# Last thirds of q and k in fewer transfers, and one closing barrier, in a cross-covariance attention kernel

## The chip, the cores and the metric

The kernel runs on one core of a Trainium2 chip. The metric is the time of one execution on the device in microseconds (us). The core has a matrix engine (PE, with its weight loads shown as PEld), a vector engine (DVE), an engine for activations and copies (ACT), GpSimd (POOL) and SyncE (SP). Sixteen DMA engines move data between the device's memory (DRAM) and the on-chip buffers. Each compute engine runs its own list of instructions in order, and engines wait for each other, and for transfers, through semaphores.

## The reference

The inputs q, k and v have shape (4, 6400, 256): four batches of 6400 rows (tokens) and 256 channels. First comes an attention over channels:

```python
qn = q / (np.linalg.norm(q, axis=1, keepdims=True) + 1e-06)
kn = k / (np.linalg.norm(k, axis=1, keepdims=True) + 1e-06)
s = kn.transpose(0, 2, 1) @ qn / tau          # 256 x 256 for each batch
s = s - s.max(-1, keepdims=True)
a = np.exp(s)
a /= a.sum(-1, keepdims=True) + 1e-09
x = v @ a                                      # 6400 x 256 for each batch
```

Then a mixture of eight experts of rank 16 is added. `w_gate` is (256, 8), `A` is (8, 256, 16), `B` is (8, 16, 256), and every row of x uses its two best experts:

```python
logits = x @ w_gate
topk = np.argpartition(-logits, K, axis=1)[:, :K]     # K = 2
w = softmax of the two chosen logits
out = x + sum over the two experts of w * ((x @ A[e]) @ B[e])
```

The 256 x 256 matrix of a batch needs all 6400 rows of q and k of that batch, so no row of the output can be computed before all of q and k of its batch has been read.

## The kernel before

**Tiles.** The 6400 rows of a batch lie on 128 partitions as 50 columns, each a row of 256 channels on every partition. A batch's q and k come in three thirds of 17, 17 and 16 columns (`QK`), its v in five pieces of 10 columns (`V`). POOL issues the loads of q, k and v, which cast from f32 to bf16 on the way, by one line, L562. The first four columns of q and k of batch 0 are an exception: SP and ACT load them as f32 (L558) and ACT casts them (L758). Of some thirds, `PARTS` cuts the transfer further:

```python
QK = ((0, 17), (17, 17), (34, 16))
PARTS = {(0, 0): ((0, 2), (2, 15)), (0, 2): ((34, 8), (42, 5), (47, 3)), (3, 2): ((34, 8), (42, 5),
        (47, 3))}
```

So the last third (columns 34 to 49) of q and of k comes in transfers of 8, 5 and 3 columns in batches 0 and 3, and in one transfer of 16 columns in batches 1 and 2.

**Stages of a batch.** For each column PE adds k'q to two accumulators (step G, L577). The squared norms of q and k come either from PE too (k'k at L581, q'q at L586) or, for the groups of columns listed in `OFF`, from ACT and DVE: ACT squares the group (L599), DVE adds it to a running sum (L605), halves that sum at the end (L611, L614), and PE sums it over the partitions (L620). After the last column ACT copies the accumulators (L635), DVE takes the diagonals (L647), computes reciprocal square roots (L661 to L677), PE spreads the scale of q (L689), ACT does the exponentials (L699), PE transposes (L713) and multiplies with the gate's and the experts' weights (L726, L729), and DVE scales the result (L741, L747). From there on the pieces of v can be turned into output: PE transposes a piece (T, L772), computes logits and expert inputs (L796, L810, L863), DVE and ACT compute the gate (L829 to L852, L874), PE transposes the gated values (L886), and the output is the sum of two products (Y, L899 and L904), which ACT or DVE copies to the tile y (L753, L755). SP stores it (L912). T and the loads of v need nothing of the attention; the other steps on v do.

**What sets the order.** A planner (`Plan.run`) plays the whole program once with assumed durations when the kernel is built, and the instructions are written in the order in which it started the steps. Each engine takes, of its ready steps, the one with the lowest rank; the steps from the last column of q and k to the scaled weights have ranks near -100 and go first. Loads go in the fixed order of `WORDS`, in which `q12` is third 2 of q and k of batch 1, and `v12` piece 2 of v of batch 1. A load starts when its buffer is free; there are six buffers for thirds of q or k and three for pieces of v. At most eight loads are outstanding: they take eight semaphores in turn, and a load waits until the load eight places before it has landed. Where the planner finds PE idle for long it puts warm-up products in (L761), which nothing reads. SP's stores of the earlier batches are held back by tiny transfers (L629) that wait until certain loads have landed (`HOLD`).

**The end.** When the kernel's function is done, the compiler's framework appends a closing block. SP waits there for all semaphores of transfers and engines. Then all engines meet in a barrier: the others raise a gather semaphore, POOL waits for all four, and raises a release semaphore that the others wait for. POOL then drains, clears the range of semaphores that the program used, and all engines meet in a second barrier of the same kind. `nc.at_finalize` lets a kernel edit the finished list of instructions, and the function `first_ahead` uses it for the first two loads.

Of the kernel before, what the change touches and what calls it, by code (L numbers as in the profile page):

```python
# [230 lines left out]
def make_plan(B, order, ahead):  # L231
# [6 lines left out]
    for kind, b, i in order:  # L238
        if kind == "v":
            p.add(("load", "v", b, i, V[i][0] * PC, V[i][1] * PC), {}, (), 0, take=(("v", (b, i)),),  # L240
                  size=LOAD * V[i][1] * PC + 0.062)
            continue
        for c, n in PARTS.get((b, i), QK[i:i + 1]):
            for h in "qk":
                p.add(("load", h, b, i, c, n), {}, (), 0, take=(("qk", (h, b, i)),), size=LOAD * n + 0.062)

    for h in "qk":
        p.add(("cast", h), {"ACT": 0.6}, [("load", h, 0, 0) + PARTS[0, 0][0]], 0)
    p.loads[2].size += 0.5
    for b in range(B):  # L250

        for i, (c0, n) in enumerate(QK):
            for c in range(c0, c0 + n):
                deps = [k for k in p.steps if k[0] == "load" and k[2:4] == (b, i) and k[1] != "v"
                        and k[4] <= c < k[4] + k[5]]
                if (b, c) < (0, PARTS[0, 0][0][1]):
                    deps = [("cast", k[1]) for k in deps]
# [32 lines left out]
        if b == 0:  # L290
            p.add(("wts",), {"DVE": 1.8}, [("load", "k", 0, len(QK) - 1) + PARTS[0, len(QK) - 1][1]], -200)

# [101 lines left out]
def make_order(words):  # L394

    order = [("qk", 0, i) for i in range(len(QK))]
    for w in words.split():
# [12 lines left out]
        (1, 1): ('k', 3, 2), (1, 2): ('k', 3, 2), (1, 3): ('k', 3, 2), (1, 4): ('k', 3, 2),  # L410
        (2, 0): ('k', 3, 1), (2, 1): ('k', 3, 2), (2, 4): ('k', 3, 1)}

PARTS = {(0, 0): ((0, 2), (2, 15)), (0, 2): ((34, 8), (42, 5), (47, 3)), (3, 2): ((34, 8), (42, 5),
        (47, 3))}
FINE = 2
FIRST = 4
OFF = {(0, 0, 'k'), (0, 0, 'q'), (0, 1, 'q'), (0, 2, 'k'), (0, 2, 'q'), (0, 4, 'q'), (0, 5, 'q'),
# [10 lines left out]
def first_ahead(nc, names):  # L428


    def move(nc):
        main, body = nc.main_func.blocks[:2]
        first = [i for i in body.instructions if i.name in names]
        assert len(first) == len(names), (names, len(first))
        rest = [i for i in body.instructions if i.name not in names]
        at = next(n for n, i in enumerate(main.instructions) if type(i).__name__ == "InstMemset")
        main.instructions = main.instructions[:at] + first + main.instructions[at:]
        body.instructions = rest
    nc.at_finalize(move)


@with_exitstack
def kernel(
# [11 lines left out]
    nc = tc.nc  # L455
# [42 lines left out]
    def make_consts():  # L498
        ident = const.tile([P, P], BF16, name="ident")
        make_identity(nc, ident)  # L500
        W["ident"] = ident
        W["ident32"] = const.tile([P, P], FP32, name="ident32")
        nc.vector.tensor_copy(W["ident32"], ident)
        ones = const.tile([P, P], FP32, name="ones")
        nc.vector.memset(ones, 1.0)
        W["ones"] = ones
        neg = const.tile([P, 1], FP32, name="neg_inv_tau")
        nc.vector.memset(neg, -inv_tau)
        W["neg"] = neg
        W["zeros"] = const.tile([P, 256], BF16, name="zeros")  # L510
        nc.vector.memset(W["zeros"], 0.0)
        nc.scalar.activation(scrap[:, 0:1], neg[0:1, :], ACT.Exp)
# [413 lines left out]
    for s in steps:  # L926
        do[s.key[0]](s, *s.key[1:])
        if s.key[0] == "load":
# [3 lines left out]
            if n_load == 4:  # L932
                make_consts()
    first_ahead(nc, {i.ins.name for i in early})


# [33 lines left out]
```

## Time and profile before

| what | value |
|---|---|
| time, median of 4 runs | 254.81 us (254.69 to 254.83) |
| time of the profiled execution | 254.82 us |
| its span, first to last instruction | 253.0 us |
| PE busy, share of the span | 217.5 us, 86% |
| DVE busy | 193.1 us, 76% |
| ACT busy | 150.6 us, 60% |
| loads of q and k, 1088 KB each | 14 issues by POOL, 23.4 us (q) and 28.1 us (k) from issue to landing |
| loads of 320 KB (5 columns) | 4 issues, 21.6 us (q) and 24.4 us (k) |
| loads of 192 KB (3 columns) | 4 issues, 22.9 us (q) and 21.6 us (k) |
| one DMA issue on POOL | 0.53 us |

The span is what the instructions of the program cover; the execution's time is longer by the work around it. The times from issue to landing include the time that a transfer waits behind others in the queue. Sizes of loads are given as they are read (f32); a page's GB/s and MB for a queue count what is written (bf16 for the casting loads). A slice of the page is a fortieth of the span, 6.3 us.

### The profile page before, as it was taken

The page shows a single profiled execution, that of the slowest core. Times are in us where ns is not written, and L with a number is a line of the kernel's source. Part 1 is how long each engine was busy: PE and PEld are TensorE (multiplying, and loading weights), DVE is VectorE, ACT ScalarE, POOL GpSimd, SP SyncE. Part 2 cuts the span into 40 slices and gives each one's busy share as a digit, 9 for nine tenths or more (in the row PEclk, how much of TensorE's full clock was granted, in tenths as well). Part 3 has the DMA queues.
Part 4 walks back from the last instruction along what each step waited for, and adds up shares of the span by engine and source line. Part 5 has one row for each costly group of instructions (what it writes and reads, how often), then busy time and mean ns, then how long its engine had stood idle before and what let it go on. Part 6 is the DMA issues. An engine that isn't in the chain of part 4 may idle for free.

```text
span 253.0 us, 5843 instructions
## 1 busy us (share of the span) xinstructions
PE 217.5 (86%) x2343; PEld 192.6 (76%) x2343; DVE 193.1 (76%) x527; ACT 150.6 (60%) x270; POOL 30.2 (12%) x58
## 2 busy tenths in 40 slices
PE   0273993899999998899999999989999869999980
PEld 0162882588989996699889998779999759999970
DVE  0055589879899978898989995689888878988920
ACT  5354436546766645877667548443776746647680
POOL 7001220040020002000030100510000210000000
PEclk9999799799999999999999999999999999999998
DMA  8999999999999999999999999999999999999995
GB/s 247 213 217 211 211 222 209 216 221 212 219 211 211 320 294 294 257 212 223 208 217 221 215 215 219 210 210 353 279 286 313 335 317 315 322 419 427 422 408 217
DMA packets 11819, 66.70 MB, mean 264 GB/s; under 512 B 1424, under 2 KB 2320, under 8 KB 7184
## 3 DMA queue, kind: packets, MB, share of 16 engines
q0 software_dynamic: 7488, 38.80, 74.6%
q1 hardware_dynamic: 3968, 26.87, 26.1%
q10 hardware_dynamic: 336, 0.66, 0.8%
q8 instruction: 18, 0.29, 0.4%
q14 instruction: 9, 0.07, 0.1%
HBM read 78.91 MB, written 26.21 MB: 415 GB/s over the span
## 4 chain that ended last, share of the span: by engine, by line
DMA 46%; PE 45%; DVE 3%; POOL 2%; issue 1%; ACT 0%; POOLq 0%
DMA qk<-in_k_dram 21%; DMA v<-in_v_dram 20%; PE Y_ps L899 12%; PE acc L577 6%; PE T_ps L772 6%; PE Y_ps L904 6%; DMA qk<-in_q_dram 4%; PE gzT_ps L886 4%; PE ZL_ps L796 3%; PE acc L586 2%; PE acc L581 2%; PE Z_ps L863 2%; POOL qk L562 1%; PE log_ps L810 1%; DVE a_bf L747 1%
## 5 line engine op out<-in xcount | busy, mean ns | idle before, releaser
L577 PE MATMUL acc<-qk 128*128 128x256 bf16 x400 | 71.4, 286 | 18.4 <-DMA qk<-in_k_dram 11.4
L605 DVE TENSOR_TENSOR ssq<-ssq,sq 128x1280 f32<-128x1280 f32 (+1 forms) x27 | 43.4, 1607 | 22.6 <-ACT sq L599 20.6
L899 PE MATMUL Y_ps<-a_bf,vT 128*128 128x256 bf16 x400 | 60.0, 273 | 0.0
L753 ACT COPY y<-Y_ps 128x512 f32<-128x512 f32 x79 | 46.0, 587 | 18.6 <-PE Y_ps L904 15.8
L599 ACT ACTIVATE sq<-qk 128x1280 f32<-128x1280 bf16 (+1 forms) x27 | 36.9, 1367 | 26.4 <-DVE ssq L605 19.7
L577 PEld LDWEIGHTS <-qk 128*128 128x128 bf16 x400 | 34.9, 103 | 22.9 <-DMA qk<-in_k_dram 13.6
L899 PEld LDWEIGHTS <-vT 128*128 128x128 bf16 x400 | 38.9, 98 | 3.9
L904 PE MATMUL Y_ps<-ball,gzT 128*128 128x256 bf16 x200 | 38.2, 273 | 0.3 <-DVE gzT L755 0.3
L581 PE MATMUL acc<-qk 128*128 128x128 bf16 x242 | 34.8, 226 | 0.0
L772 PE MATMUL T_ps<-ident,v 128*128 128x128 f32 x200 | 27.1, 276 | 1.6 <-DVE gatemask L839 0.9
L562 POOL DMA_DIRECT2D v<-in_v_dram x20 | 12.2, 612 | 128.8 <-PE T_ps L772 81.8
L581 PEld LDWEIGHTS <-qk 128*128 128x128 bf16 x242 | 24.5, 101 | 3.7
L753 ACT COPY vT<-T_ps 128x512 f32<-128x512 f32 (+1 forms) x44 | 21.7, 516 | 9.2 <-PE T_ps L772 8.8
L874 DVE TENSOR_TENSOR gz<-zl,gateg 128x256 bf16<-128x256 f32 x70 | 26.0, 446 | 0.3
L772 PEld LDWEIGHTS T_ps<-ident,v 128*128 128x128 f32 x200 | 22.3, 143 | 3.1 <-DMA v<-in_v_dram 1.1
L586 PE MATMUL acc<-qk 128*128 128x128 bf16 x168 | 23.6, 223 | 0.0
L904 PEld LDWEIGHTS <-gzT 128*128 128x128 bf16 x200 | 19.4, 98 | 3.0 <-DVE gzT L755 0.6
L796 PE MATMUL ZL_ps<-waA_sb,vT 128*128 128x136 bf16 x280 | 19.6, 222 | 1.3 <-DVE waA_sb L741 0.9
L886 PE MATMUL gzT_ps<-ident,gz 128*128 128x128 f32 x100 | 20.4, 278 | 0.0
L796 PEld LDWEIGHTS <-vT 128*128 128x128 bf16 x280 | 17.8, 98 | 2.1 <-issue 1.7
L755 DVE COPY gzT<-gzT_ps 128x256 f32<-128x256 f32 (+1 forms) x39 | 14.9, 390 | 4.5 <-PE gzT_ps L886 4.0
L599 ACT ACTIVATE ssq<-qk 128x1536 f32<-128x1536 bf16 x8 | 11.9, 1484 | 8.1 <-DMA qk<-in_q_dram 3.9
(80 smaller groups left out, 269.8 us busy)
## 6 DMA issues: line engine op xcount, KB each, us to landing
out_dram<-y SPq DMA_DIRECT2D x18, 1280.0 KB, 17.9
v<-in_v_dram POOLq DMA_DIRECT2D x20, 640.0 KB, 20.5
qk<-in_q_dram POOLq DMA_DIRECT2D x7, 1088.0 KB, 23.4
qk<-in_k_dram POOLq DMA_DIRECT2D x7, 1088.0 KB, 28.1
qk<-in_q_dram POOLq DMA_DIRECT2D x2, 1024.0 KB, 18.2
qk<-in_k_dram POOLq DMA_DIRECT2D x2, 1024.0 KB, 22.7
out_dram<-y SPq DMA_DIRECT2D x4, 512.0 KB, 6.2
qk<-in_q_dram POOLq DMA_DIRECT2D x2, 512.0 KB, 16.9
```

The source lines that it names most:

```text
L577: nc.tensor.matmul(acc[ic][:, 0:256], kt[:, j, ic::CC], qt[:, j, :], start=c == 0, stop=False, skip_group_check=True)
L581: nc.tensor.matmul(acc[ic][:, 256:384], kt[:, j, ic::CC], kt[:, j, ic::CC], start=False, stop=False, skip_group_check=True)
L586: nc.tensor.matmul(acc[ic][:, 384:512], qt[:, j, ic * P:(ic + 1) * P], qt[:, j, ic * P:(ic + 1) * P], start=False, stop=c == NC - 1, skip_ ...
L599: nc.scalar.activation(out[:, 0:n, :], t[:, j:j + n, :], ACT.Square)
L605: nc.vector.tensor_tensor(out=t, in0=t, in1=held["sq", (w, b, g), ""][:, 0:n, :], op=OP.add)
L753: nc.scalar.copy(out, in_)
L772: nc.tensor.matmul(ps[:, j, :], vt[:, c + j, :].bitcast(FP32), W["ident32"], is_transpose=True, start=(j == 0), stop=(j == n - 1))
L796: nc.tensor.matmul(ps[:, j, :], vT_of(b, i, c + j)[:, :, ic], st[b]["waA"][:, ic, :], start=(j == 0 and ic == 0), stop=(j == n - 1 and ic ...
L874: nc.vector.tensor_tensor(out=pairs[:, h].rearrange("p c (e r) -> p c e r", e=E), in0=z[:, 2 * h:2 * h + 2, :].rearrange("p c (e r) -> p c ...
L886: nc.tensor.matmul(ps[:, j, :], pairs[:, j * P:(j + 1) * P], W["ident32"], is_transpose=True, start=(j == 0), stop=(j == n // 2 - 1))
L899: nc.tensor.matmul(ps[:, j, :], vT_of(b, i, c + j)[:, :, ic], st[b]["a"][:, ic, :], start=(j == 0 and ic == 0), stop=False, skip_group_che ...
L904: nc.tensor.matmul(ps[:, j, :], pair[:, :, j], W["B"], start=False, stop=(j == 1), skip_group_check=True)
```

## The change

Two edits. First, `PARTS`: the last thirds of q and k in batches 0 and 3 come in two transfers of 8 columns each, in place of 8, 5 and 3. Second, a new function `one_end_barrier` edits the closing block: it removes POOL's release of the first barrier, all of the second barrier of the other engines, and POOL's gather wait of the second, so that POOL gathers, drains, clears the semaphores, drains and then releases the others once.

```diff
-PARTS = {(0, 0): ((0, 2), (2, 15)), (0, 2): ((34, 8), (42, 5), (47, 3)), (3, 2): ((34, 8), (42, 5),
-        (47, 3))}
+PARTS = {(0, 0): ((0, 2), (2, 15)), (0, 2): ((34, 8), (42, 8)), (3, 2): ((34, 8), (42, 8))}
...
+def one_end_barrier(nc):
+
+
+    def trim(nc):
+        end = nc.main_func.blocks[-1]
+        ins = list(end.instructions)
+        pool = [n for n, i in enumerate(ins) if i.engine == mybir.EngineType.Pool]
+        clear = next(n for n in pool if type(ins[n]).__name__ == "InstISA")
+        before = [n for n in pool if n < clear and type(ins[n]).__name__ == "InstEventSemaphore"]
+        after = [n for n in range(clear + 1, len(ins))]
+        release = [n for n in after if n in pool and type(ins[n]).__name__ == "InstEventSemaphore"]
+        assert len(before) == 2 and len(release) == 2 and len(after) == 11, (before, release, after)
+        drop = {before[-1]} | {n for n in after if n != release[-1] and n != release[0] - 1}
+        end.instructions = [i for n, i in enumerate(ins) if n not in drop]
+    nc.at_finalize(trim)
...
             if n_load == 4:
                 make_consts()
     first_ahead(nc, {i.ins.name for i in early})
+    one_end_barrier(nc)
```

The planner reads `PARTS`, so the order of the program changes too. In the built program POOL has four loads fewer, PE 14 warm-up products more (2337 products in place of 2323), and from the end of batch 0's columns on the lists of PE, DVE and ACT differ in most places. At the end of batch 0, ACT now copies the first accumulator before its last square rather than after it, DVE takes the diagonals before the two reductions rather than between them, and PE adds 12 columns of batch 1 rather than 5 before it spreads the scale of q. On SP the first store goes ahead of the first holding transfer, and the third holding transfer goes ahead by one store.

## The prediction

> **What bounds the kernel now.** I read first the page's second and third parts (the span in 40 slices, and the DMA queues).
>
> ```profile
> span 253.0 us, 5843 instructions
> ...
> DMA  8999999999999999999999999999999999999995
> GB/s 247 213 217 211 211 222 209 216 221 212 219 211 211 320 294 294 257 212 223 208 217 221 215 215 219 210 210 353 279 286 313 335 317 315 322 419 427 422 408 217
> ...
> q0 software_dynamic: 7488, 38.80, 74.6%
> q1 hardware_dynamic: 3968, 26.87, 26.1%
> ...
> HBM read 78.91 MB, written 26.21 MB: 415 GB/s over the span
> ```
>
> The DMA row is full in every slice but the first and the last. The casting loads (q0) and the stores (q1) together hold 74.6 + 26.1 = 100.7% of the sixteen engines' span. The drop from 420 to 210 GB/s is no idling: a casting load reads four bytes for each two that it writes, and only the written ones are counted. So no wait elsewhere sets the end unless it leaves the DMA queue empty.
>
> Second, the busy time by stage, for who sets the last microseconds.
>
> ```profile
> core 0: us, PE busy (x) PEld busy (x) DVE busy (x) ACT busy (x) POOL busy (x), PEclk, DMA share, GB/s
> ...
> 24.00:36.00 12.00, 11.46 (x118) 10.36 (x119) 7.43 (x13) 5.51 (x4) 3.36 (x6) 0.86 1.09 214
> 36.00:60.00 24.00, 18.82 (x193) 14.98 (x191) 20.62 (x59) 13.33 (x22) 3.47 (x5) 0.93 1.04 215
> 224.00:246.00 22.00, 21.73 (x237) 19.66 (x235) 16.54 (x56) 15.91 (x33) 0.00 (x0) 1.00 1.00 419
> 246.00:248.00 2.00, 0.00 (x0) 0.00 (x0) 0.00 (x0) 0.35 (x1) 0.00 (x0) 1.00 1.02 409
> 248.00:250.00 2.00, 0.00 (x0) 0.00 (x0) 0.00 (x0) 0.00 (x0) 0.00 (x0) 1.00 0.77 311
> 250.00:252.00 2.00, 0.00 (x0) 0.00 (x0) 0.00 (x0) 0.00 (x0) 0.00 (x0) 0.64 0.28 112
> ```
>
> PE works to the last product (it ends at 245.74), the last store is issued at 246.38, and then the DMA engines run down unevenly: all busy to 248, 0.77 of them to 250, 0.28 to 252. In the trace's landing records the sixteen completions of that last store come in from 248.87 to 252.14. The quickest engines thus had nothing queued before it; the slowest was still 252.14 - 248.87 = 3.27 us behind, with DMA work alone. So the slowest engine's queue sets the end, and PE has about 3.3 us in hand.
>
> Third, the closing rows and the waits of POOL, which issues all loads but the first two.
>
> ```profile
> L965 POOLq EVENT_SEMAPHORE  x4: 17/17/17, 252.3 to 252.9; - x4
> L965 POOLq DRAIN  x3: 40/93/19034, 207.0 to 252.8; - x3
> ...
> POOL v L562 <- PE T_ps L772: 81.8, 10, 20.6
> POOL qk L562 <- ACT ssq L599: 16.6, 1, 16.6
> ```
>
> POOL waits long for buffers, but with transfers queued behind it: at 158.17, after its 16.6 us for ACT, a k transfer of 1088 KB was still due to land at 166.81; the shortest cover I found is at 198.83, where the transfer before landed at 205.26, 6.4 us later.
>
> **The change, part by part.** The sum is made against the profiled execution: 254.82 us, span 253.04, so 1.78 around it; the median of the runs is 254.81, the same.
>
> *Closing barrier.* Starts from the trace, POOL's sequencer: gather wait 252.314, release 252.392, drain 252.473, range clear 252.595, drain 252.768, second gather wait 252.853, release 252.931; the other engines take the release from 252.973 and the span ends at 253.036. The edit takes two links out of this chain: the first release (252.392 to 252.473, 0.08) and the second gather wait (252.853 to 252.931, 0.08). Nothing runs beside them. The other engines' second drains were over by 252.61, ahead of POOL: nothing. Sum: -0.16 us. Bounds 0 (should the last drain wait longer) and -0.24 (a third such link).
>
> *Four transfers fewer.* 5 + 3 columns in two transfers become 8 in one, for q and k, in batches 0 and 3. The bytes stay. Removed are 4 x 128 = 512 packets, 512/16 = 32 per engine. In the trace's packet records a packet of 2560 written bytes takes 211 ns, one of 1536 takes 135, one of 4096 on the same queue 324: 211 + 135 - 324 = 22 ns, times 32 = 0.70 us. That is the upper bound, because packets overlap: the window of 24 to 36, where the small ones run, shows a DMA share of 1.09. The landings give the net price. Back to back, 10 columns (v, 640 KB) come 3.04 us apart, and 17 columns (1088 KB) 5.18: (5.18 - 3.04)/7 = 0.306 a column, leaving 3.04 - 3.06 = nothing per transfer. Batch 0's two small pieces of q and of k, 16 columns in four transfers, took 5.01 us (first completions, from 28.54 of the transfer before to 33.55 of the last); 16 x 0.306 = 4.90. Four transfers cost 0.11 there, and two fewer save about half, 0.06; I allow 0.07 for each batch. Sum: -0.14, bounds 0 and -0.70. I take the landings over the packet times, since they are what a waiting engine sees.
>
> The Trainium skill, "DMA: Bandwidth & Descriptors", section "Anatomy of one DMA", gives each GpSimd-issued transfer a fixed 2.0 us besides its bytes; charged in full for four transfers it would be an estimate of 8 us and a time near 246.7. The spacing above shows no such charge while the queue is full, so the measurement decides and the rule counts only for a lone transfer.
>
> *POOL's issues.* Four DMA issues of 0.53 us fall away, and two waits: before, the fifth transfer of q in batch 0 (issued 10.51) and of k (14.46) waited for a free semaphore of eight; now eight transfers are issued at once. Later loads wait for an earlier neighbour by two. But the next q load at 20.48 waits for its buffer (PE), unchanged, and the queue is full until 35. Worth nothing, hidden by 14 us of queued transfers.
>
> *Later data.* Columns 42 to 46 of k now arrive with 47 to 49, near 34.9 instead of 33.16. PE then has 8 columns of 0.33 us (the 28.85 to 32.5 rows) ahead of it: 34.9 + 2.7 + 0.3 for the start = 37.9, against 37.3 now. In the changed program ACT's copy of the accumulator stands ahead of the last square, so that square moves from 37.58 to about 38.4. On DVE the diagonal sums (0.84) and the two reductions (1.84 each) follow in another order; the row scales, ready at 47.3 now, come near 48.3: +1.0 us for batch 0's softmax. Its cover: at 50.44, when the next v load is issued, transfers are queued until 64.90. In batch 3, column 42 starts near 181 and the last column ends at 192.9, while all of q and k has landed at 183.40: PE's order decides there, not the landing. Nothing on the path, as long as PE ends before 245.74 + 3.27 = 249.0.
>
> *New order.* The planner moves most instructions of PE, DVE and ACT after batch 0, and puts in 14 more warm-up products. Six of them take 1.46 us at 40.01 (0.22 from start to start): 14 x 0.22 = 3.1 if they stand before waiting work, nothing if PE is idle there; most stand in the wait for batch 0's sums (PE busy 18.82 of 24.00 in 36 to 60). I take 0 to 1 us on PE, inside the 3.3.
>
> Total: 254.82 - 0.16 - 0.14 = 254.52, so **254.5**; its own range 253.96 (both full) to 254.66 (barrier alone).
>
> **Rivals.**
>
> *The packets pay in full.* For it: 32 packets less on every engine, and the slowest engine sets the end. Against it: the share over 1, which says that a packet's fixed part runs under its neighbour. 254.82 - 0.16 - 0.70 = 253.96.
>
> *PE becomes the bound at the end.* The mechanism: a PE that starts batch 0's output later stays late, because it is full afterwards (21.73 of 22.00 in the stage above), and the last store is issued after the slowest engine would have run dry. It decides from a PE end of 249.0. Its price: 1.0 for the chain, 3.1 for the warm-up products if they all stand before work, makes 4.1, or 0.8 past the cover; if the five later columns also cost batch 3 their 5 x 0.44 = 2.2 (the spacing of full columns at 172.33 to 174.55), 3.0. Less the barrier: 255.5 to 257.7, of which I take 255.5. For it: the changed order of everything. Against it: PE sits idle for 2.2 us in 200 to 210, which can take up lateness.
>
> *Nothing happens.* The queue's gain is lost in the uneven run-down of the engines and the last drain takes the barrier's: 254.8. For it: a single 16 KB instruction fetch takes 0.9 us of one engine, as much as the whole gain.
>
> **How the numbers follow.** This kernel's measurement can tell about 0.2% (0.51 us) from no change: faster is below 254.30, slower above 255.32. My forecast has 0.38, packets in full 0.33, PE bound 0.22, nothing 0.07. The forecast and nothing lie within 0.2% but for 0.02 at the fast edge: faster 0.35, same 0.43, slower 0.22. The range starts below the full packets by the run-down's play of 0.25 and ends at the PE rival's near price: 253.7 to 255.6.
>
> **What would show it.** Barrier right: one release in the closing rows, and 0.73 us in place of 0.89 from the last landing to the end of the span. Packets: four fewer landings, and the last q and k of batch 0 landing 0.05 to 0.35 us sooner than 35.01. Cover right: the DMA share at 0.99 or more up to 246, and PE's end below 249.0. Wrong: a stage with a DMA share under 0.97 before 246, a last completion that comes in with the first (PE bound), or a batch 0 chain late by more than 3 us.

## The result and the profile after

| | before | after |
|---|---|---|
| time, median | 254.78 us (61 runs, 254.60 to 254.93) | 254.39 us (41 runs, 254.21 to 254.65) |
| span of the profiled execution | 253.04 us | 252.56 us |
| last landing | 252.14 | 251.83 |
| end of PE's last product | 245.7 | 246.3 |

The ratio is 0.9985, with a 95% interval from 0.9981 to 0.9990: 0.39 us less, between 0.26 and 0.48. Forecast were 254.5, 0.30 us less than before, and a range from 253.7 to 255.6. The spans, landings and ends of PE in the table are those of one profiled execution of each kernel.

The page of the kernel after, its DMA rows:

```profile
span 252.6 us, 5852 instructions
...
DMA  8999999999999999999999999999999999999996
GB/s 253 210 218 209 215 224 209 212 224 214 214 213 213 319 292 290 263 213 221 210 215 217 218 219 215 211 212 318 312 253 342 332 332 316 347 385 428 406 408 242
DMA packets 11244, 66.70 MB, mean 264 GB/s; under 512 B 1361, under 2 KB 1745, under 8 KB 6609
...
q0 software_dynamic: 6912, 38.80, 74.4%
```

The same bytes move in 7488 - 6912 = 576 packets fewer: the 512 that carry data and 64 completions. The queue's own time falls from 74.6% of 253.04 to 74.4% of 252.56 us. The DMA row is as full as before.

The closing rows of the kernel after (instructions of one line: engine, count, shortest, middle and longest time in nanoseconds, first and last start; the lines of this kernel are numbered 16 or 17 higher than those of the kernel before):

```profile
L982 POOLq DRAIN  x3: 40/102/13032, 213.2 to 252.4; - x3
L982 SPq DRAIN  x2: 7/7/7, 251.9 to 252.0; - x2
L982 POOLq EVENT_SEMAPHORE  x2: 17/17/17, 252.0 to 252.5; - x2
```

POOL has two semaphore instructions there in place of four. From the last landing to the end of the span it is 252.56 - 251.83 = 0.74 us, where it was 0.89.

The stage from 238 to 240 of the kernel before, and the last stages of the kernel after (busy us of each engine, clock, DMA share, GB/s):

```profile
238.00:240.00 2.00, 2.00 (x21) 1.72 (x19) 1.99 (x7) 0.82 (x3) 0.00 (x0) 1.00 1.02 424
```

```profile
238.00:240.00 2.00, 2.00 (x27) 1.87 (x25) 2.00 (x7) 0.96 (x2) 0.00 (x0) 1.00 0.87 363
...
246.00:248.00 2.00, 0.32 (x3) 0.04 (x1) 0.00 (x0) 0.87 (x2) 0.00 (x0) 1.00 1.03 407
248.00:250.00 2.00, 0.00 (x0) 0.00 (x0) 0.00 (x0) 0.00 (x0) 0.00 (x0) 1.00 0.83 334
250.00:252.00 2.00, 0.00 (x0) 0.00 (x0) 0.00 (x0) 0.00 (x0) 0.00 (x0) 0.56 0.20 78
```

PE ends 0.6 us later than before, and at 238 to 240 the DMA engines were not all busy (0.87, where it was 1.02). Yet the last landing is 0.31 us earlier. The sixteen completions of the last store come in from 249.48 to 251.83, 2.35 us apart where it was 3.27. The first of them comes 2.5 us after the store is issued in both kernels (246.38 to 248.87, 246.97 to 249.48), so the narrower distance follows PE's later end; the slowest engine did not lose by it.

### The profile page after: what moved, and what is told of

It reads as the page before. It is cut to its first block, busy times and chain, and to the rows that moved or that the text cites. A ratio compares the mean times of both kernels' runs of the same rounds, so it can differ in the third digit from the quotient of the medians.

```text
span 252.6 us, 5852 instructions
## 1 busy us (share of the span) xinstructions
PE 221.1 (88%) x2357; PEld 195.2 (77%) x2357; DVE 192.8 (76%) x528; ACT 151.2 (60%) x269; POOL 27.1 (11%) x54
## 3 DMA queue, kind: packets, MB, share of 16 engines
q0 software_dynamic: 6912, 38.80, 74.4%
## 4 chain that ended last, share of the span: by engine, by line
PE 76%; DVE 9%; DMA 8%; ACT 2%; issue 2%; POOL 1%; DVEq 0%; POOLq 0%
PE Y_ps L915 17%; PE acc L593 16%; PE Y_ps L920 8%; DMA qk<-in_k_dram 8%; PE T_ps L788 7%; PE ZL_ps L812 6%; PE gzT_ps L902 5%; PE acc L597 5%; PE acc L602 4%; PE warm_ps L777 2%; PE n2p_ps L636 2%; DVE a_bf L763 2%; PE Z_ps L879 1%; PE log_ps L826 1%; DVE a_exp L663 1%
## 5 line engine op out<-in xcount | busy, mean ns | idle before, releaser
L593 PEld LDWEIGHTS <-qk 128*128 128x128 bf16 x400 | 35.4, 104 | 20.5 <-DMA qk<-in_k_dram 10.4
L615 ACT ACTIVATE sq<-qk 128x1280 f32<-128x1280 bf16 (+1 forms) x27 | 36.9, 1368 | 17.5 <-DVE ssq L621 16.6
L597 PEld LDWEIGHTS <-qk 128*128 128x128 bf16 x242 | 24.7, 102 | 3.8
L578 POOL DMA_DIRECT2D v<-in_v_dram x20 | 11.5, 576 | 132.6 <-PE T_ps L788 119.1
L771 DVE COPY y<-Y_ps 128x512 f32<-128x512 f32 x21 | 14.5, 700 | 4.1 <-PE Y_ps L920 4.1
```

Source lines behind the costliest of these rows:

```text
L593: nc.tensor.matmul(acc[ic][:, 0:256], kt[:, j, ic::CC], qt[:, j, :], start=c == 0, stop=False, skip_group_check=True)
L597: nc.tensor.matmul(acc[ic][:, 256:384], kt[:, j, ic::CC], kt[:, j, ic::CC], start=False, stop=False, skip_group_check=True)
L615: nc.scalar.activation(out[:, 0:n, :], t[:, j:j + n, :], ACT.Square)
L771: nc.vector.tensor_copy(out, in_)
```

## The experiments

Each kernel was timed against the kernel before on the same chip; e1 to e4, e5 to e8 and e9 to e11 each ran together.

**e1: the closing barrier alone.** The kernel before with `one_end_barrier` and its call, nothing else.

> The kernel before with the closing barrier edited and nothing else; every engine's order and all transfers are those of before. My theory: two links of 0.08 us leave POOL's closing chain, 0.16 us less than before, so about 254.62 if before is at 254.78; the time from the last landing to the end of the span falls from 0.89 to about 0.74. Rival (the last drain waits longer, or the work after the span takes it back): no difference, 254.78. If the whole gain of 0.39 us were the barrier's: 254.39.

254.65 us against 254.84: 0.19 less, ratio 0.9992 (0.9984 to 1.0001). The interval just reaches no difference, but the profiles settle the size: last landing 252.15, end 252.87, 0.72 us. In the eight profiled kernels with the old closing block (before, e2 to e7, e11) this stretch is 0.89 to 0.91 us, in four with the new one (after, e1, e8, e9) 0.72 to 0.74.

**e2: `PARTS` alone.** The kernel after without the call of `one_end_barrier`.

> The changed kernel with the old closing block: the 8 + 8 transfers and the new order alone. My theory: 0.39 - 0.16 = 0.23 us less than before, 254.55. Rival (packets pay in full, and something else gives part of it back): 0.4 to 0.7 less. Rival (the barrier did all): no difference, 254.78.

254.74 us against 254.84: 0.10 less, ratio 0.9996 (0.9987 to 1.0005). 0.4 to 0.7 less is outside the interval (0.33 less at most); no difference is not.

**e3: new transfers in the old order.** Planned with 8, 5 and 3; every engine's list of compute steps and SP's list are those of before.

```diff
+        if what != "v" and i == 2 and c == 42:
+            n = 8
+        if what != "v" and i == 2 and c == 47:
+            return
         nc.gpsimd.dma_start(t[:, c - c0:c - c0 + n, :], src[b, :, c:c + n, :])
```

> The kernel before, planned with transfers of 8, 5 and 3 columns, so that every engine's order is that of before, but the 5 and the 3 are issued as one transfer of 8. My theory (a transfer's net price is 0.035 us, four fewer): 0.14 us less than before, 254.64. Rival (the packets' own times count in full): 0.70 less, 254.08. Rival (the new order did it): no difference, 254.78.

254.68 us against 254.84: 0.16 less, ratio 0.9992 (0.9983 to 1.0001). 0.70 less is excluded (0.43 at most).

**e4: old transfers in the new order.** Planned with 8 + 8, without the new barrier.

```diff
-        nc.gpsimd.dma_start(t[:, c - c0:c - c0 + n, :], src[b, :, c:c + n, :])
+        for c, n in ((42, 5), (47, 3)) if what != "v" and i == 2 and c == 42 else ((c, n),):
+            nc.gpsimd.dma_start(t[:, c - c0:c - c0 + n, :], src[b, :, c:c + n, :])
```

> The changed order (planned with 8 + 8) with the old closing block, but each last transfer of 8 issued as 5 and 3 columns. My theory: the order is worth nothing, because PE has about 3.3 us in hand at the end: as before within 0.15, 254.78. Rival (the order gave the gain, by spreading the end more evenly over the DMA engines: the completions of the last store come in within 2.35 us in place of 3.27): 0.1 to 0.3 less. Rival (the order costs, since PE ends 0.58 later, and the transfers pay for it): up to 0.58 more.

254.85 us against 254.84, ratio 1.0002 (0.9993 to 1.0011). So no cost or gain of the new order is seen (at most 0.28 more, 0.18 less), though PE ends at 246.8 and the completions of the last store are 2.26 us apart. Before, e3, e4 and e2, all with the old closing block, form a square: old order 254.84 and 254.68, new order 254.85 and 254.74. The new transfers save 0.16 and 0.11, the new order costs 0.01 and 0.06; each of these is smaller than its interval of about 0.2 either way.

The traces read the transfers more sharply. In batch 0, take the first of the sixteen completions of the 8 columns of k, and the first completion of the last columns of k; 16 columns lie between. In the seven profiles with four transfers there (before, e1, e4 to e7, e11) this takes 5.01 to 5.03 us, in the five with two (after, e2, e3, e9, e10) 4.88 to 4.93. Two transfers fewer save about 0.11 us. The last completions, which PE waits for, scatter too much to show it (5.22 to 5.60 and 5.25 to 5.59 for the same stretch), and so do those of batch 3 (all of q and k landed at 182.96 to 184.06 with the old transfers, 182.79 to 183.46 with the new).

**e5: twenty transfers more.** Every v load in two halves.

```diff
-        nc.gpsimd.dma_start(t[:, c - c0:c - c0 + n, :], src[b, :, c:c + n, :])
+        for c, n in ((c, 5), (c + 5, 5)) if what == "v" else ((c, n),):
+            nc.gpsimd.dma_start(t[:, c - c0:c - c0 + n, :], src[b, :, c:c + n, :])
```

> The kernel before, same order on all engines, with each of the twenty loads of v issued as two transfers of 5 columns: 20 transfers more, 160 packets more on each DMA engine. By the net price of 0.035 us a transfer: 0.7 us more, 255.5. By the packets' own time (22 ns each): 3.5 us more, 258.3. By a fixed 2.0 us for each transfer in line: 40 us more. If less than half as much is queued (eight transfers at most are outstanding), the DMA queue could run dry, and the share by stage would show it.

264.01 us against 255.00: 9.0 more, ratio 1.0364 (1.0347 to 1.0381). No price expected gives this. A stage of the kernel before, and the stages of e5, show where it is:

```profile
200.00:224.00 24.00, 21.79 (x268) 19.59 (x267) 20.07 (x64) 13.22 (x36) 1.88 (x2) 1.00 1.03 334
```

```profile
200.00:224.00 24.00, 15.36 (x120) 12.57 (x121) 9.52 (x33) 6.39 (x19) 3.03 (x5) 0.64 1.04 347
224.00:234.00 10.00, 10.00 (x128) 9.53 (x126) 8.86 (x25) 6.31 (x16) 0.00 (x0) 1.00 1.00 297
234.00:240.00 6.00, 6.00 (x82) 5.58 (x81) 5.29 (x19) 3.14 (x7) 0.00 (x0) 1.00 0.37 155
240.00:246.00 6.00, 6.00 (x61) 5.51 (x59) 5.48 (x20) 3.98 (x8) 0.00 (x0) 1.00 0.65 273
```

From 200 to 224 the DMA engines are full (1.04), and PE stands idle for want of v (busy 15.36 of 24.00, before 21.79): the last piece lands at 233.3, where it was 223.8. Afterwards PE is full and the DMA engines wait for stores (0.37). This looks like loads and stores moved in the wrong proportion, and not like the transfers' own cost; e11 tests it. The queues from 188 to 200 (packets, MB, share of sixteen engines), first before, then e5:

```profile
q0 software_dynamic: 279, 1.29, 52.5%
q1 hardware_dynamic: 305, 2.48, 50.8%
```

```profile
q1 hardware_dynamic: 385, 3.29, 67.2%
q0 software_dynamic: 382, 0.86, 36.9%
```

The two queues move about as many packets each (279 to 305, 382 to 385; without the small completion packets 252 to 242 and 337 to 321). With packets of half the size the loads got 0.86 MB in place of 1.29. If the queues take one packet each in turn, a piece of v needs 8 pairs of 399 + 398 ns on every engine before, an estimate of 6.4 us, and 16 pairs of 211 + 398 ns in e5, 9.7 us. Before, the pieces came 6.1 us apart; in e5 the halves came 4.7 apart, 9.4 a piece: nearly the same ratio. The load queue was not dry, as the expectation had allowed for: five or six loads were issued and not landed at 188, 194, 200, 206 and 212, before two.

**e11: only the first thirteen pieces of v in halves.** As e5, with `what == "v" and (b, i) < (2, 3)`; the last seven, which run beside the stores, stay whole.

> As e5, but only the first 13 pieces of v (batches 0 and 1, and three of batch 2) go as two transfers of 5 columns; the last seven, which share the DMA engines with the stores from 186 to 224 us, stay whole. My theory now: a transfer itself costs 0.03 to 0.04 us, so 0.4 to 0.6 more, 255.2 to 255.6 if before is at 254.8; e5's 9 us come from the last seven, whose smaller packets get a smaller share beside the stores' packets. Rival (every further transfer costs alike): 13/20 of e5's 9.0 us, 5.9 more, 260.7.

255.44 us against 254.80: 0.64 more, ratio 1.0025 (1.0016 to 1.0034). That is 0.64/13 = 0.05 us a transfer (0.03 to 0.07), and e5's other 8.4 us, the difference of the two runs, come with the last seven pieces. The stage of e11 where e5 lost PE's time:

```profile
200.00:224.00 24.00, 21.99 (x268) 19.66 (x267) 20.55 (x65) 13.53 (x36) 1.81 (x3) 1.00 1.03 330
```

**e6 and e7: PE's last product late.** The kernel before with 8 or 24 products that nothing reads, into the bank of the last product for y.

```diff
         ps = bank(s, ("Y", b, i, c), [P, 2, C], FP32)
+        for _ in range(8 if (b, i, c) == (B - 1, NP - 1, 8) else 0):
+            nc.tensor.matmul(ps.rearrange("p a b -> p (a b)"), W["ident"], W["zeros"][:, None, :].to_broadcast([P, 2, 256]),
+                             start=True, stop=True)
```

> The kernel before with 8 products that nothing reads put in front of PE's last product for y, so that PE ends and the last store is issued 8 x 0.216 = 1.7 us later. My theory (the slowest DMA engine still has 3.3 us of queued work when the last store comes): 0 to 0.3 us more, 254.8 to 255.1. Rival (PE and the last store set the end): 1.7 more, 256.5.

> The same with 24 products, 5.2 us later. My theory: what is past the cover of 3.3 us shows, 1.9 us more, 256.7, and the completions of the last store come in close together. Rival (PE and the last store set the end): 5.2 more, 260.0.

e6: 254.93 us against 255.00, ratio 1.0004 (0.9995 to 1.0014), so at most 0.36 more. The last store is issued at 247.51 in place of 246.38 and lands at 252.02. It is 1.13 us later and not 1.7; PE's end also moves between runs of one order (245.15 to 245.73 in before, e1, e3 and e9). e7: 255.85 us, 0.85 more, ratio 1.0031 (1.0020 to 1.0043). Its stages and its last transfer:

```profile
248.00:250.00 2.00, 2.00 (x13) 1.02 (x12) 0.00 (x0) 0.00 (x0) 0.00 (x0) 1.00 0.60 236
250.00:252.00 2.00, 0.47 (x5) 0.18 (x2) 0.00 (x0) 0.59 (x1) 0.00 (x0) 1.00 0.11 44
252.00:254.00 2.00, 0.00 (x0) 0.00 (x0) 0.00 (x0) 0.00 (x0) 0.00 (x0) 0.97 0.33 124
```

```profile
out_dram<-y SPq DMA_DIRECT2D x1, 256.0 KB, 2.0
```

Here the DMA engines are nearly dry when the last store comes (0.11), and PE does set the end. Issued at 251.12, the store lands 2.0 us later, where the queue of before made it 5.8. So PE's cover in the kernel before is 252.14 - 2.0 - 246.38 = 3.76 us. The issue is 4.74 later, 4.74 - 3.76 = 0.98 past the cover, and the span grew by 254.05 - 253.04 = 1.01. These two agree by construction, since the 2.0 comes from the same trace; the times of the nine runs are the check from outside, 0.85 more (0.51 to 1.10).

**e8: one transfer of 16 columns.** The kernel after with `((34, 16),)` for both batches (and `PARTS[..][-1]` where the planner reads the last part).

> The changed kernel with the last thirds of batches 0 and 3 in a single transfer of 16 columns: four transfers fewer again, new order again. By the price of a transfer alone: 0.14 us less than the changed kernel, 254.25. Against it: batch 0's columns 34 to 49 of k all come near 34.9, PE then has 16 columns ahead of it, 16 x 0.33 = 5.3 us, and batch 0's softmax is 2.6 us later than in the changed kernel, near the end of PE's cover: if that cover is used up, 255 to 257.

254.97 us against 255.00, ratio 1.0003 (0.9991 to 1.0014), with runs from 254.23 to 255.58; so the gain of the kernel after is gone in the median. In the profiled execution PE did not take it. There is a stage with idle DMA engines, and yet the last landing is at 251.73, earlier than in the kernel after:

```profile
238.00:246.00 8.00, 8.00 (x76) 7.26 (x74) 4.71 (x16) 6.71 (x14) 0.00 (x0) 1.00 0.88 361
```

PE ends at 247.0 and the last store is issued at 247.62, 4.1 us before it lands; by e7's 2.0 us PE still had 2.1 us in hand, so the cover was not used up. Over the twelve runs the median span is 252.65 us, against 253.2 in the kernel before beside it. What grew is the time around the span: 1.75 to 2.78 us, in the median 2.05, where all other kernels have 1.73 to 1.93. The spans scatter too (252.4 to 253.5). What causes either stays open.

**e9: the change without its new order.** The kernel of e3 with `one_end_barrier`.

> The order of before, the 5 and 3 columns issued as one transfer of 8, and the one closing barrier: the change without its new order. My theory (the order is worth nothing): as the changed kernel, 0.3 to 0.4 us less than before. Rival (the new order gave part of it, by its closer completions of the last store): 0.15 to 0.25 us less only.

254.46 us against 254.80: 0.34 less, ratio 0.9987 (0.9978 to 0.9995), as the kernel after (0.9985). The interval reaches from 0.13 to 0.56 less, so it does not exclude the rival's 0.15 to 0.25.

**e10: the last stores steered.** As e9, with the last two stores in 120 and 8 partitions.

```diff
-        nc.sync.dma_start(out_v[b, :, lo:lo + n, :], held["y", (b, i), ""][:, c:c + n, :])
+        for p0, p1 in ((0, 120), (120, P)) if (b, i) == (B - 1, NP - 1) and c else ((0, P),):
+            nc.sync.dma_start(out_v[b, p0:p1, lo:lo + n, :], held["y", (b, i), ""][p0:p1, c:c + n, :])
```

> As e9, but the last two stores (4 and 2 columns) go as 120 and 8 partitions each, so that one of the sixteen DMA engines should get none of the 120. The Trainium skill, DMA: Bandwidth & Descriptors, section Why a DMA increments its semaphore by 16 and not by 1, says that a transfer's engines are the largest count up to 16 that divides the partitions, 15 for 120, the lowest-numbered ones; by its section Latency and other measured facts engines 7 and 15 are often the slow ones. If one engine alone is last, and it is the one left out, the last landing comes up to 0.4 us sooner (the two stores are 8 x (0.16 + 0.08) = 1.9 us of an engine's work, but in the profile of before the next engines are only 0.1 to 0.6 us behind the last). If several engines are last together, as the share of 0.28 from 250 to 252 says: no gain, or 0.1 to 0.5 more for the two added transfers.

254.89 us against 254.80, ratio 1.0003 (0.9994 to 1.0012), where e9 had 0.9987. The last landing is at 251.95 as in e9 (251.93), so no single engine left out this way was alone at the end; which engines are last the records don't say. The span ends 1.16 us after it, in e9 0.72, and that is the whole loss against e9 (0.43 us). In the closing block SP waits for the eight semaphores of its transfers in a fixed order. In e9 the last landing is on the last of them. In e10, with two stores more, it is on the first, and the seven other waits come after it, 0.06 us each, from 251.97 to 252.39.

## Why the prediction was right

**The bound.** The slowest DMA engine's queue sets the end. e6 and e7 show it: PE 1.1 us late costs nothing that the runs can tell (at most 0.36), 4.7 us late costs 0.85, about what lies past the cover. The cover was read as 3.27 us, from the quickest engine's completion; it is 3.76, because a lone store of 256 KB lands 2.0 us after its issue and not 2.5 (e7): the quickest engines, too, had some work queued.

**The barrier, -0.16.** Measured 0.89 - 0.74 = 0.16 in the profile after (with the unrounded ends), 0.17 in that of e1, and 0.19 by time in e1.

**The transfers, -0.14.** The mechanism held, the size was somewhat low. The first completions give 0.11 us for batch 0, or 0.055 a transfer (e11: 0.05), where 0.07 was allowed; twice that would be 0.22, if batch 3 saved as much, which no run shows. There the small pieces run beside stores (43.0% of the DMA engines' time between 169 and 184 us), so the size of the packets could count too. By time it is 0.16 and 0.11 in the square of e1 to e4, and 4 x 0.05 = 0.20 by e11. e3 also holds what POOL saves with four issues fewer; the two are not told apart. The choice between landings (0.035 a transfer) and packet times (0.18) was the step that mattered: e3 and e11 exclude the packet times. That choice was argued from landings as what a waiting engine sees, but the sum used the first of sixteen completions, and an engine waits for the last (before, PE starts at 14.23 on a load of k whose completions come from 13.28 to 14.18). By the last ones the same stretch of the kernel before takes 5.58 us, which would have priced four transfers at 0.68. They scatter too much to price anything, so the first ones were the better reading, but not for the reason given.

The forecast sign for the packets proves nothing either. The last q and k of batch 0 land at 34.83 in place of 35.01, inside the forecast 0.05 to 0.35, but the transfer before them was already 0.19 earlier (29.24, before 29.43), and over all profiles the old transfers end at 34.72 to 35.01, the new ones at 34.73 to 34.93. The rule of the Trainium skill weighed there, a fixed 2.0 us for each transfer ("DMA: Bandwidth & Descriptors", "Anatomy of one DMA"), is not seen with a full queue: thirteen transfers more cost 0.64 us in e11. For a lone load of POOL no run here tests it.

**The order, nothing.** e4, and e9 against the kernel after, show no effect, to about 0.2 or 0.3 us. The step on batch 0's softmax had the wrong cause. Forecast was that the row scales would be ready 1.0 us later, at 48.3; they were ready at 47.6. What came later was PE: it had twelve columns of batch 1 ahead of the scale of q, a difference that stood in the description of the change and was left out of this step. The kernel before and the kernel after, PE and then DVE:

```profile
45.45 2.06 PE L577 MATMUL acc<-qk 128*128 128x256 bf16 x10 [0.87 <-DMA qk<-in_k_dram]
47.47 1.19 PE L689 MATMUL rq_ps<-rqI,ones 128*128 128x256 f32 x2
...
49.57 0.75 DVE L694 TENSOR_TENSOR acc_sb<-acc_sb,rq_ps 128x256 f32<-128x256 f32 x2
```

```profile
45.71 3.19 PE L593 MATMUL acc<-qk 128*128 128x256 bf16 x14
...
50.56 0.65 PE L705 MATMUL rq_ps<-rqI,ones 128*128 128x256 f32 x2
...
51.24 0.75 DVE L710 TENSOR_TENSOR acc_sb<-acc_sb,rq_ps 128x256 f32<-128x256 f32 x2 [1.90 <-PE rq_ps L705]
```

DVE's step is 1.7 us late, not 1.0. That nothing came of it at the end is right by the cover, not by this step: PE ends at 246.3 to 246.8 with the new order (after, e2, e4) and at 245.1 to 245.7 with the old, a difference well within 3.76 us.

**The sign that misled.** A DMA share under 0.97 before 246 was named as a sign of a wrong forecast. It came (0.87 in 238 to 240), and the forecast held. The share is a mean of sixteen engines. That the ones that idle there are those with time in hand fits the end of the span, but the trace does not name the engines. e4 has the same dip (0.88) and no cost is seen.

**The rivals.** Packets in full: excluded. PE as the bound: real, but past 3.76 us (e7). Nothing: excluded by the interval of the whole change.

The parts add up: 0.19 (e1) and 0.16 (e3) make 0.35, and by the traces 0.16 and 0.22 make 0.38; e9 has 0.34, the kernel after 0.39 with an interval of 0.26 to 0.48. The forecast of 0.30 was a little low, and the term that was too small is the transfers'.

## What to carry to other kernels

Here the DMA engines were full from end to end: a delay of PE within its cover cost nothing that could be told, and a transfer removed was worth what the spacing of completions said, not what its packets lasted. Compare completions of the same rank among the sixteen: the first ones agreed to 0.05 us between runs, the last ones only to 0.4. Ask how far each engine is behind at the end: a mean share hides that a few of the sixteen finish last, and the cover of everything else is measured against those. Before cutting transfers finer, look whether another queue runs beside them.

## What the runs showed of the hardware

- Two DMA queues that both had work queued moved about equal numbers of packets, as if one packet each in turn, so a queue's share went with the size of its packets: halving the packets of the loads cut them from 52.5% to 36.9% of the engines' time between 188 and 200 us, and 8.4 us of e5's 9.0 came with the loads that ran beside stores.
- Packets of casting loads overlapped: a packet of 1536 written bytes lasts 135 ns, but the stage with small packets has a DMA share of 1.09, and thirteen transfers more, 104 packets more on each engine, cost 0.64 us, or 6 ns a packet, where their lengths would say 23 (two of 2560 bytes last 2 x 211, one of 5120 lasts 399). Batch 0's two transfers fewer agree: 0.11 us for 16 packets on each engine, or 7 ns.
- In before, after, e1 to e4 and e9 the sixteen completions of the last store lie 2.3 to 3.8 us apart (2.26 in e4, 3.76 in e1), though it has 128 partitions to spread over the engines. The last one moved by 0.5 us between these kernels (251.75 to 252.27); the first came 2.5 to 2.6 us after the issue in each, so most of the 1.5 us by which the distance differs is PE's end.
- In the closing block a wait of SP for a semaphore that is already there takes 0.06 us, a semaphore link of POOL 0.08. The order of the waits counts: the same last landing with seven waits behind it cost 0.43 us in e10.
